# Turning the first attention head's Q and K by identity matmuls and by halves, with a mask bias in three operations

## The chip, the cores and the metric

One core of a Trainium2 chip. The metric is the device time of one execution in microseconds. The profile gives a span (first to last instruction); in nearly all runs the time is the span plus 1.8 us. Ratios are the mean time of one kernel's runs over that of the other's runs of the same rounds, so they are not quite the ratio of the medians that are quoted.

## The reference

```python
scores = scale * np.matmul(q, k.transpose(0, 1, 3, 2))      # 4 batches, 8 heads, 768 x 64
mask = window of +-1 block | first and last block | 3 sampled blocks for each of 24 query blocks
scores = np.where(mask, scores, -1e9); attn = softmax(scores)
x = attn @ v                                                 # to (4, 768, 512)
u = x + low_rank_mix(x, U, V)
out = u + np.maximum(u @ w_ch1, 0) @ w_ch2
```

## The kernel before

A pair of heads takes 12 score steps: two matmuls of 384 columns, an exponential on ACT (ScalarE), and later the product with V on PE. The mask rides in the contraction: rows 0 to 63 hold Q or K, 24 more rows hold the block's one-hot code on the query side and its bias (0 or -240) on the key side. Before the first step, Q and K of head 0 have to be loaded, cast to FP16, turned on PE, and copied to these rows. The bias has to be computed from the sampled blocks, spread over the keys by a matmul, and copied too. This start-up is what the change touches. `keep_warm` issues matmuls of zeros ("fillers") that only keep PE busy.

```python
    def first_turn(h, n):                       # n = 0: Q, 1: K
        pt = psm([P, S], FP16)
        for t in range(T):                      # 6 transposes of 128 columns
            nc.tensor.transpose(
                out=pt[0 : (h + 1) * D, t * P : (t + 1) * P],
                in_=sts[0, ("qld", "kld")[n]][:, t, 0 : h + 1].rearrange("p h d -> p (h d)"),
                identity=id16,
            )
        return pt
    def first_rows(h, n, pt, copy):             # one copy of the whole row, 768 columns
        copy(out=(qres, kres)[n][0][drows[h], h, :], in_=pt[drows[h], :])
# ... in the start-up, each engine in this order (memsets cut):
        keep_warm(8)
        nc.scalar.copy(out=qres[0][mrows[0], 0, :], in_=ohT)
        first_cast(0, 0, nc.vector.tensor_copy)
        ptq = first_turn(0, 0)
        keep_warm(1)
        prev = ms
        for r in range(3):                      # a01 = max(mask, sampled == block), 3 times
            nc.vector.scalar_tensor_tensor(...)
        nc.vector.tensor_scalar(out=bias..., scalar1=-MASK_BIAS, scalar2=MASK_BIAS, ...)
        first_rows(0, 0, ptq, nc.vector.tensor_copy)
        first_cast(0, 1, nc.scalar.copy)
        # two mask matmuls, 24 rows, 384 columns each, into pks[0], pks[1]  (cut)
        first_rows(0, 1, first_turn(0, 1), nc.scalar.copy)
        keep_warm(3)
        # four mask rows copied, (head 0, half 1) on ACT, the others on DVE  (cut)
```

The softmax here doesn't subtract the row's maximum and nothing guards it: scores larger than these inputs give would overflow.

## Time and profile before

303.17 us, median of 3 runs (302.99 to 303.46) when the prediction was made. The profiled execution had a span of 303.4 us and a time of 305.13. That is 2 us above the other three.

| stage of the profiled run | us | what leads |
|---|---|---|
| start-up | 0 to 8.8 | casts, turns, mask, copies in a chain |
| batch 0 | 8.8 to 54 | the exponentials on ACT |
| the rest | 54 to 303.4 | PE, busy nearly all the time |

The first lines below are the page's busy times. The others are from the view of three stretches: for each its length, then busy time and (in brackets) instructions of PE, of its weight loads, of DVE, ACT and POOL, then the granted clock, the DMA share and GB/s.

```profile
PE 295.6 (97%) x2760; PEld 181.1 (60%) x2760; DVE 141.6 (47%) x298; ACT 182.4 (60%) x261; POOL 49.7 (16%) x69
```

```profile
0.00:8.80 8.80, 7.61 (x26) 2.87 (x27) 5.80 (x14) 3.73 (x5) 3.16 (x11) 1.00 0.68 200
8.80:54.00 45.20, 43.12 (x588) 30.45 (x587) 28.35 (x63) 43.03 (x59) 26.34 (x35) 1.00 1.01 280
54.00:303.40 249.40, 244.86 (x2153) 147.83 (x2149) 107.49 (x223) 135.64 (x199) 20.22 (x25) 1.00 0.43 102
```

After the start-up ACT is busy 43.0 of 45.2 us, and PE about as much. Later PE alone has no room. So a gain at the start of the exponentials goes through to the end, unless something later eats it.

Now the start-up: PE, then ACT, by the timeline (start, duration of the merged group, engine, line, operation, output<-input, rows*columns of the weights, rows x columns of the moving side, count, and idle time before it with its releaser).

```profile
4.71 0.85 PE L188 MATMUL pm<-id_94,stqld 128*64 128x128 f16 x6
5.49 0.61 PE L209 MATMUL psc<-warm 128*128 128x512 f16 x1
6.03 0.50 PE L231 MATMUL pv<-small,bias 24*128 24x384 f16 x1
6.33 0.52 PE L231 MATMUL pm<-small,bias 24*128 24x384 f16 x1
6.78 0.85 PE L188 MATMUL pm<-id_94,stkld 128*64 128x128 f16 x6
7.56 1.46 PE L209 MATMUL psc<-warm 128*128 128x512 f16 x3
8.81 0.85 PE L327 MATMUL psc<-qres_102,kres_104 128*128 128x384 f16 x2
9.45 0.85 PE L188 MATMUL pm<-id_94,stqld 128*128 128x128 f16 x6
10.09 0.75 PE L327 MATMUL psc<-qres_102,kres_104 128*128 128x384 f16 x2
10.68 0.50 PE L188 MATMUL pm<-id_94,stkld 128*128 128x128 f16 x6
```

```profile
7.66 0.79 ACT L196 COPY kres_104<-pm 64x768 f16<-64x768 f16 x1 [2.47 <-PE pm L188]
8.48 0.47 ACT L241 CAST kres_104<-pm 24x384 f16<-24x384 f32 x1
9.70 0.81 ACT L333 ACTIVATE est<-psc 128x768 f16<-128x768 f32 x1 [0.74 <-PE psc L327]
10.88 3.77 ACT L333 ACTIVATE est<-psc 128x768 f16<-128x768 f32 x5 [0.37 <-PE psc L327]
```

The same six 128-column transposes take 0.85 us at 9.45 and 0.50 at 10.68; one by one their starts are 107 and 56 ns apart. PE's clock opens from half to full in between. The trace's own record of the granted clock begins its stretch of full speed at 10.61 us. The page's clock row shows 9 throughout and the view of the first stretch 1.00. Neither tells this, so it has to be read from the spacing of matmuls. The first exponential starts at 9.70, and the second waits 0.37 us for slow matmuls.

### The profile page before, as it was taken

How to read it: one execution, taken by the hardware profiler on the slowest of the kernel's cores; microseconds unless marked ns; L12 is line 12 of the kernel's file. 1: busy time of each engine (PE TensorE's matmuls, PEld its weight loads, DVE VectorE, ACT ScalarE, POOL GpSimd, SP SyncE). 2: the span in 40 equal slices, each digit the busy share in tenths (PEclk: the TensorE clock that was granted, in tenths of full speed). 3: DMA queues.
4: the chain of work that ended last, by engine and by line, in shares of the span. 5: the costliest groups of instructions: out<-in, count | busy, mean ns of one | idle time of the engine just before them, and what ended most of it. 6: DMA issues, size and time to landing. Idle time of an engine off the chain costs nothing.

```text
span 303.4 us, 6760 instructions
## 1 busy us (share of the span) xinstructions
PE 295.6 (97%) x2760; PEld 181.1 (60%) x2760; DVE 141.6 (47%) x298; ACT 182.4 (60%) x261; POOL 49.7 (16%) x69
## 2 busy tenths in 40 slices
PE   8999999999999999999999999999999999999994
PEld 3566766666666556666665556566665555665441
DVE  7466766546553533445462523446463435443121
ACT  3899999577766665777776555677776530332000
POOL 3691493222221111020201001000000000000000
PEclk9999999999999999999999999999999999999999
DMA  6999989979966476461946162431500121000111
GB/s 186 328 295 240 328 254 236 279 176 187 219 195 139 143 162 177 103 167 26 159 71 136 49 143 77 110 72 28 104 18 22 62 61 71 35 0 2 69 69 70
DMA packets 58519, 39.96 MB, mean 132 GB/s; under 512 B 40136, under 2 KB 54872, under 8 KB 58488
## 3 DMA queue, kind: packets, MB, share of 16 engines
q1 hardware_dynamic: 55764, 35.32, 44.4%
q0 software_dynamic: 2688, 4.19, 7.6%
q8 instruction: 21, 0.34, 0.4%
q14 instruction: 10, 0.08, 0.1%
q10 hardware_dynamic: 36, 0.01, 0.0%
HBM read 27.72 MB, written 6.29 MB: 112 GB/s over the span
## 4 chain that ended last, share of the span: by engine, by line
PE 89%; ACT 7%; DVE 2%; issue 1%; ACTq 0%
PE pm L447 27%; PE pm L469 27%; PE psc L327 17%; PE pv L366 10%; ACT est L333 7%; PE psc L209 2%; PE pm L388 1%; PE pm L419 1%; PE pm L188 1%; DVE xh L380 1%; DVE xf L380 0%; PE pm L465 0%; PE pm L435 0%; DVE of L477 0%; PE pm L314 0%
## 5 line engine op out<-in xcount | busy, mean ns | idle before, releaser
L333 ACT ACTIVATE est<-psc 128x768 f16<-128x768 f32 x192 | 151.5, 810 | 54.8 <-PE psc L327 53.7
L469 PE MATMUL pm<-w2t,tT 128*128 128x512 f16 x384 | 94.1, 379 | 0.0
L366 PEld LDWEIGHTS <-est 128*128 128x128 f16 x1152 | 55.4, 97 | 23.1 <-DVE xf L380 3.4
L447 PEld LDWEIGHTS <-w1t 128*128 128x128 f16 x512 | 46.3, 98 | 25.3
L457 DVE TENSOR_SCALAR tT<-pm 128x384 f16<-128x384 f32 x64 | 35.6, 556 | 51.5 <-PE pm L447 37.7
L455 ACT ACTIVATE tT<-pm 128x384 f16<-128x384 f32 x64 | 31.4, 491 | 35.8 <-PE pm L447 17.0
L469 PEld LDWEIGHTS <-tT 128*128 128x128 f16 x384 | 34.1, 98 | 30.7
L327 PE MATMUL psc<-qres_102,kres_104 128*128 128x384 f16 x192 | 47.4, 329 | 1.2 <-ACT est L333 1.0
L327 PE MATMUL psc<-qres_103,kres_105 128*128 128x384 f16 x192 | 46.7, 326 | 0.6 <-ACT est L333 0.4
L477 DVE TENSOR_TENSOR of<-xf,pm 128x512 f32<-128x512 f32 x24 | 16.4, 684 | 30.5 <-PE pm L469 30.5
L366 PE MATMUL pv<-vt_98,est 128*128 128x65 f16 x576 | 30.3, 193 | 0.2
L366 PE MATMUL pv<-vt_99,est 128*128 128x65 f16 x576 | 30.5, 193 | 0.1
L327 PEld LDWEIGHTS <-kres_104 128*128 128x128 f16 x192 | 18.2, 98 | 14.3 <-issue 2.1
L327 PEld LDWEIGHTS <-kres_105 128*128 128x128 f16 x192 | 18.1, 98 | 14.1 <-issue 0.8
L375 DVE RECIPROCAL rcp<-pv 128x6 f32<-128x6 f32 x32 | 6.2, 193 | 37.4 <-PE pv L366 37.3
L380 DVE TENSOR_TENSOR xh<-pv,rcp 128x384 f16<-128x384 f32 x32 | 17.8, 557 | 1.0
L380 DVE TENSOR_TENSOR xf<-pv,rcp 128x384 f32<-128x384 f32 x32 | 17.5, 547 | 0.0
L425 DVE TENSOR_TENSOR xf<-xf,pm 128x384 f32<-128x384 f32 x24 | 13.1, 546 | 0.0
L140 POOL CAST qst_100<-qld 128x768 f16<-128x768 f32 x5 | 4.1, 828 | 44.9 <-DMA qres_102<-qst_100 44.8
L140 POOL CAST qst_101<-qld 128x768 f16<-128x768 f32 x5 | 4.2, 831 | 43.8 <-DMA qres_103<-qst_101 43.8
L447 PE MATMUL pm<-uT_3047,w1t 128*128 128x384 f16 x32 | 10.4, 326 | 0.0
L447 PE MATMUL pm<-uT_3048,w1t 128*128 128x384 f16 x32 | 10.4, 326 | 0.0
(118 smaller groups left out, 300.4 us busy)
## 6 DMA issues: line engine op xcount, KB each, us to landing
vld<-in_v_dram SPq DMA_DIRECT2D x16, 384.0 KB, 7.2
out_dram<-of SPq DMA_DIRECT2D x24, 256.0 KB, 2.0
qld<-in_q_dram SPq DMA_DIRECT2D x15, 384.0 KB, 3.9
kld<-in_k_dram SPq DMA_DIRECT2D x15, 384.0 KB, 6.6
w1t<-in_moe_w_ch_dram POOLq DMA_DIRECT2D x4, 512.0 KB, 10.0
w2t<-in_moe_w_ch_dram POOLq DMA_DIRECT2D x4, 512.0 KB, 12.1
qld<-in_q_dram SPq DMA_DIRECT2D x2, 192.0 KB, 3.5
kld<-in_k_dram SPq DMA_DIRECT2D x2, 192.0 KB, 4.6
```

The costliest lines, as they stand in the source:

```text
L140: last = nc.gpsimd.tensor_copy(out=dst, in_=ld)
L327: nc.tensor.matmul(psc[:, c, 0:HS], kT[:, h, g * P : (g + 1) * P], qT[:, h, c * HS : (c + 1) * HS], start=True, stop=True,)
L333: nc.scalar.activation(out=est.rearrange("k (c n) -> k c n", c=2), in_=psc[:, :, 0:HS], func=AF.Exp, scale=0.125,)
L366: nc.tensor.matmul(pav[:, sc, :], est[:, sc * P : (sc + 1) * P], vts[self.b % 2][:, head, g, 0 : D + 1], start=(g == 0 and sc == 0), stop= ...
L375: nc.vector.reciprocal(out=rcp, in_=pav[:, :, D])
L380: nc.vector.tensor_tensor(out=dst, in0=pav[:, :, 0:D], in1=rcp[:, :, None].broadcast_to([P, T, D]), op=ALU.mult,)
L425: nc.vector.tensor_add(out=xf, in0=xf, in1=pu)
L447: nc.tensor.matmul(pt, w1t[:, cc, jj * P : (jj + 1) * P], bt.uT[cc][:, c * HS : (c + 1) * HS], start=(cc == 0), stop=(cc == NCC - 1),)
L455: nc.scalar.activation(out=dst, in_=pt, func=AF.Relu)
L457: nc.vector.tensor_scalar_max(out=dst, in0=pt, scalar1=0.0)
L469: nc.tensor.matmul(hold[sc], bt.tT[jj][:, sc * P : (sc + 1) * P], w2t[:, jj, :], start=(b > 0 and jj == 0), stop=(jj == NJJ - 1),)
L477: nc.vector.tensor_add(out=of, in0=bt.xf[:, sc, :], in1=hold[sc])
```

## The change

Turn Q and K of the first head by ordinary matmuls against the identity, into FP32 PSUM, in two halves of 384 columns; put K ahead of the mask and drop the filler before it; copy the halves on DVE and ACT side by side; shorten the last fillers; compute the bias in three operations. A likely reason for matmuls in place of transposes: the Trainium skill ("TensorE: Matmul & The Clock Gate", Part 4) says that transposes do not count as PE activity for the clock.

```diff
-        [ms_np.view(np.float16), ...]
+        [((ms_np - 1.0) * -MASK_BIAS).view(np.float16), ...]
-    def first_turn(h, n):                      # 6 transposes into one FP16 tile
+    def first_turn(h, n, c):                   # half c: 3 matmuls into an FP32 tile
+            nc.tensor.matmul(pt[0:D, j * P : (j + 1) * P],
+                sts[0, ("qld", "kld")[n]][:, 3 * c + j, h], id16,
+                start=(j == 0), stop=(j == 2), skip_group_check=True)
 ...
         keep_warm(8)
         first_cast(0, 0, nc.vector.tensor_copy)
-        ptq = first_turn(0, 0)
-        keep_warm(1)
-        (bias in 4 operations)
-        first_rows(0, 0, ptq, nc.vector.tensor_copy)
-        first_cast(0, 1, nc.scalar.copy)
-        (two mask matmuls)
-        first_rows(0, 1, first_turn(0, 1), nc.scalar.copy)
-        keep_warm(3)
-        (four mask rows, one on ACT)
+        first_turn(0, 0, 0)
+        first_turn(0, 0, 1)
+        (bias in 3 operations: compare with all 3 samples, reduce by max, scale and max)
+        first_cast(0, 1, nc.scalar.copy)
+        first_turn(0, 1, 0)
+        first_row(0, 0, nc.vector.tensor_copy)
+        first_row(0, 1, nc.scalar.copy)
+        mask_half(0)
+        first_row(1, 0, nc.scalar.copy)
+        first_turn(0, 1, 1)
+        mask_half(1)
+        keep_warm(2, 256)
+        mask_row(0, 0, nc.vector.tensor_copy)
+        first_row(1, 1, nc.vector.tensor_copy)
+        (the other three mask rows on DVE)
```

More of the change, by code (lines that the diff above doesn't have):

```diff
@@ L69 @@
     small_np = np.concatenate(
-        [ms_np.view(np.float16), ii[:, None].astype(np.float32).view(np.float16), ohT_np],
+        [
+            ((ms_np - 1.0) * -MASK_BIAS).view(np.float16),
+            ii[:, None].astype(np.float32).view(np.float16),
+            ohT_np,
+        ],
         axis=1,
@@ L174 @@
     bias = consts.tile([P, 2, D], FP16)
-    a01 = consts.tile([P, NB], FP32)
     for vt in vts:
@@ L183, in first_cast @@
         copy(out=sts[0, nm][:, :, h], in_=lds[nm][:, h])
-    def first_turn(h, n):
-        pt = psm([P, S], FP16)
-        for t in range(T):
-            nc.tensor.transpose(
-                out=pt[0 : (h + 1) * D, t * P : (t + 1) * P],
-                in_=sts[0, ("qld", "kld")[n]][:, t, 0 : h + 1].rearrange("p h d -> p (h d)"),
-                identity=id16,
-            )
-        return pt
-    def first_rows(h, n, pt, copy):
-        copy(out=(qres, kres)[n][0][drows[h], h, :], in_=pt[drows[h], :])
+    first_out = {}
+    def first_turn(h, n, c):
+        if n == 1:
+            pt = psm([P, HS], FP32)
+        elif c == 0:
+            pt = pw[:, 1, 0:HS]
+        else:
+            pt = pscp.tile([P, 2, 512], FP32, tag="psc", name="psc")[:, 0, 0:HS]
+        first_out[n, c] = pt
+        for j in range(3):
+            nc.tensor.matmul(
+                pt[0:D, j * P : (j + 1) * P],
+                sts[0, ("qld", "kld")[n]][:, 3 * c + j, h],
+                id16,
+                start=(j == 0), stop=(j == 2), skip_group_check=True,
+            )
     with tc.manual_schedule(
@@ L205, with keep_warm, mask_half @@
         pw = pscp.tile([P, 2, 512], FP32, tag="psc", name="psc")
-        def keep_warm(n):
+        def keep_warm(n, cols=512):
             for _ in range(n):
-                nc.tensor.matmul(pw[:, 0], warm[:, 0:P], warm, start=True, stop=True)
-        keep_warm(8)
-        nc.scalar.copy(out=qres[0][mrows[0], 0, :], in_=ohT)
-        first_cast(0, 0, nc.vector.tensor_copy)
-        ptq = first_turn(0, 0)
-        keep_warm(1)
-        prev = ms
-        for r in range(3):
-            nc.vector.scalar_tensor_tensor(
-                out=a01[0:NB], in0=sb[0:NB, :, r, 0], scalar=iota,
-                in1=prev, op0=ALU.is_equal, op1=ALU.max,
-            )
-            prev = a01[0:NB]
-        nc.vector.tensor_scalar(
-            out=bias[0:NB, :, 0:NB], in0=a01[0:NB, None].broadcast_to([NB, 2, NB]),
-            scalar1=-MASK_BIAS, scalar2=MASK_BIAS, op0=ALU.mult, op1=ALU.add,
-        )
-        first_rows(0, 0, ptq, nc.vector.tensor_copy)
-        first_cast(0, 1, nc.scalar.copy)
+                nc.tensor.matmul(
+                    pw[:, 0, 0:cols], warm[:, 0:P], warm[:, 0:cols], start=True, stop=True
+                )
         pks = [psvp.tile([P, HS], FP32, tag="pv", name="pv"), psm([P, HS], FP32)]
-        for c in range(2):
+        def mask_half(c):
             nc.tensor.matmul(
@@ L236, with mask_row @@
             )
-        first_rows(0, 1, first_turn(0, 1), nc.scalar.copy)
-        keep_warm(3)
-        for h in range(2):
-            for c in range(2):
-                (nc.scalar.copy if (h, c) == (0, 1) else nc.vector.tensor_copy)(
-                    out=kres[0][mrows[h], h, c * HS : (c + 1) * HS], in_=pks[c][mrows[h]]
-                )
-        nc.vector.tensor_copy(out=qres[0][mrows[1], 1, :], in_=ohT)
+        def mask_row(h, c, copy):
+            copy(out=kres[0][mrows[h], h, c * HS : (c + 1) * HS], in_=pks[c][mrows[h]])
@@ new lines, in first_row @@
+        def first_row(n, c, copy):
+            copy(
+                out=(qres, kres)[n][0][drows[0], 0, c * HS : (c + 1) * HS],
+                in_=first_out[n, c][0:D],
+            )
+        keep_warm(8)
+        nc.scalar.copy(out=qres[0][mrows[0], 0, :], in_=ohT)
+        first_cast(0, 0, nc.vector.tensor_copy)
+        first_turn(0, 0, 0)
+        first_turn(0, 0, 1)
+        eq = consts.tile([P, NB, 3], FP32)
+        a01 = consts.tile([P, NB], FP32)
+        nc.vector.tensor_scalar(
+            out=eq[0:NB], in0=sb[0:NB, :, :, 0], scalar1=iota, scalar2=-1.0,
+            op0=ALU.is_equal, op1=ALU.add,
+        )
@@ new lines @@
+        nc.vector.tensor_reduce(
+            out=a01[0:NB], in_=eq[0:NB], axis=mybir.AxisListType.X, op=ALU.max
+        )
+        nc.vector.scalar_tensor_tensor(
+            out=bias[0:NB, :, 0:NB], in0=a01[0:NB, None].broadcast_to([NB, 2, NB]),
+            scalar=-MASK_BIAS, in1=ms[:, None].broadcast_to([NB, 2, NB]),
+            op0=ALU.mult, op1=ALU.max,
+        )
+        first_cast(0, 1, nc.scalar.copy)
+        first_turn(0, 1, 0)
+        first_row(0, 0, nc.vector.tensor_copy)
+        first_row(0, 1, nc.scalar.copy)
@@ new lines, with last_turn @@
+        mask_half(0)
[5 more added lines that the diff above has]
+        first_row(1, 1, nc.vector.tensor_copy)
+        mask_row(0, 1, nc.vector.tensor_copy)
+        mask_row(1, 0, nc.vector.tensor_copy)
+        mask_row(1, 1, nc.vector.tensor_copy)
+        nc.vector.tensor_copy(out=qres[0][mrows[1], 1, :], in_=ohT)
+    def last_turn(n):
+        pt = psm([P, S], FP16)
+        for t in range(T):
+            nc.tensor.transpose(
+                out=pt[:, t * P : (t + 1) * P],
+                in_=sts[0, ("qld", "kld")[n]][:, t].rearrange("p h d -> p (h d)"),
+                identity=id16,
+            )
+        nc.vector.tensor_copy(
+            out=(qres, kres)[n][0][drows[1], 1, :], in_=pt[drows[1], :]
+        )
@@ L246, in first_front @@
     def first_front(n):
         first_cast(1, n, nc.gpsimd.tensor_copy)
-        first_rows(1, n, first_turn(1, n), nc.vector.tensor_copy)
+        last_turn(n)
     def second_set():
```

## The prediction

> **What bounds the kernel now.** The busy table gives PE 97% of the 303.4 us span, ACT and DVE 60% and 47%. The chain of waits has four stages. Up to about 9.7 us it is start-up. From there to about 54 us the softmax exponentials on ACT lead (0.81 us each, starting every 0.7 to 0.8 us). From 54 us the matmuls follow without a gap. The change touches only the start-up, so a gain is what it takes off the start of the exponentials; I see no stall later that would swallow it (the POOL casts of the next pairs finish ahead of their use).
>
> **Before, from the timeline.** Q cast ends 4.65; six Q transposes 4.72 to 5.56; bias by four DVE operations 4.57 to 5.56; mask matmuls end 6.53 and 6.85; six K transposes 6.78 to 7.63; ACT copies the whole K row (0.79 us) until 8.46; three 512-column filler matmuls hold PE until 8.81; first scores 8.81; first exponential 9.70. The second starts only at 10.88, 0.37 us late, because Q transposes and scores run at half clock: 512-column matmuls start 427 ns apart, 128-column ones 107 ns; after 10.6 us 56 ns.
>
> **Costs of the change.** Three bias operations instead of four: about 5.45 instead of 5.56 (estimate from 0.24 us per operation plus 48 more elements). K no longer stands behind filler and mask: its cast ends at 5.19, so half 0 of K is turned by 5.88 and mask half 0 by about 6.25. Copies from FP32 PSUM cost more: 0.55 us for 384 columns on DVE, as 768 FP16 columns cost now; but DVE and ACT share them. DVE: Q half 0 until 6.05, mask row until 6.84. ACT: Q half 1 until 6.1, K half 0 until 6.6. Data of the first scores ready at 6.9 instead of 8.5. PE's order (two matmul turns, two masks, two 256-column fillers, 0.21 us each at half clock) frees it at about 7.25. So the first scores start about 1.55 us earlier. The other mask rows and K half 1 end on DVE by 9.2, before they are needed.
>
> **Clock.** The Trainium skill ("TensorE: Matmul & The Clock Gate", Part 4) says that transposes don't count as PE activity, and Part 1 that the clock opens after a busy window of about 3.4 us. This trace fits: matmuls from 1.19 us, with 12 transposes among them, opened it only at 10.6. With real matmuls throughout it should open near 7.2, one window earlier. Then scores take 0.16 us each half, the second exponential follows the first at once (about 7.7 and 8.4), and the gain at the second is 2.4 us. If the clock still opens at 10.6, the second starts at 9.4, and the third is held again: about 0.9 us stay.
>
> **Predicted time.** Two thirds for the early clock: 300.7; else 302.2. I say 301.0, range 300.3 to 302.4. Chances: faster by over 2% 0.01, within 2% 0.98, slower 0.01.
>
> **What would show it.** Timeline: first scores near 7.2 (confirming the shorter chain), first exponential near 7.7, no gap before the second, matmul starts 56 ns apart for 128 columns before 8.5 us (confirming the clock). Chain of waits: filler and scores at the start, no ACT copy of K. From 54 us on the same durations, all shifted.
>
> **What would make it wrong.** Column- or row-weighted activity, so that 64-column and 24-row matmuls don't count either; a clock window of another phase; POOL's second K cast (waits for its DMA, ended 8.16) or pair 1's casts (10.56) becoming what PE waits for, since PE takes them in order; the mask row copies on DVE longer than read; the schedule after 54 us not passing the shift on.

## The result

302.56 us, median of 6 runs (302.19 to 302.66), against 303.31 (302.99 to 305.11, 6 runs) before: ratio 0.9965, 95% interval 0.994 to 0.9989. The class is "same", as forecast, but the time lies outside the predicted range (302.4 at most), and the gain is 0.75 us where 2.2 were forecast.

The profile, taken alone, says the opposite: its span fell from 303.4 to 300.4 us, 3 us, rather more than forecast. First the busy times and the stretches, then PE, ACT and one line of DVE, as above.

```profile
PE 292.7 (97%) x2758; PEld 180.2 (60%) x2758; DVE 142.4 (47%) x299; ACT 181.7 (60%) x261; POOL 49.6 (17%) x69
```

```profile
0.00:6.70 6.70, 5.50 (x24) 2.35 (x25) 5.13 (x13) 3.47 (x5) 2.40 (x9) 1.00 0.63 179
6.70:52.00 45.30, 43.23 (x594) 30.52 (x593) 30.70 (x67) 43.38 (x59) 28.27 (x38) 1.00 1.01 285
52.00:300.40 248.40, 243.92 (x2144) 147.28 (x2141) 106.61 (x221) 134.88 (x198) 18.91 (x23) 1.00 0.43 104
```

```profile
4.72 0.79 PE L200 MATMUL psc<-id_94,stqld 128*64 128x128 f16 x6
5.35 0.35 PE L200 MATMUL pm<-id_94,stkld 128*64 128x128 f16 x3
5.63 0.33 PE L225 MATMUL pv<-small,bias 24*128 24x384 f16 x1
5.89 0.35 PE L200 MATMUL pm<-id_94,stkld 128*64 128x128 f16 x3
6.18 0.33 PE L225 MATMUL pm<-small,bias 24*128 24x384 f16 x1
6.44 0.39 PE L218 MATMUL psc<-warm 128*128 128x256 f16 x2
6.70 0.48 PE L371 MATMUL psc<-qres_102,kres_104 128*128 128x384 f16 x2
7.02 0.50 PE L281 MATMUL pm<-id_94,stqld 128*128 128x128 f16 x6
```

```profile
5.55 0.47 ACT L236 CAST qres_102<-psc 64x384 f16<-64x384 f32 x1 [0.26 <-PE psc L200]
5.92 0.47 ACT L236 CAST kres_104<-pm 64x384 f16<-64x384 f32 x1
7.22 7.42 ACT L377 ACTIVATE est<-psc 128x768 f16<-128x768 f32 x10 [0.83 <-PE psc L371]
```

```profile
6.00 0.56 DVE L233 CAST kres_104<-pv 24x384 f16<-24x384 f32 x1 [0.16 <-PE pv L225]
```

Everything in the forecast chain is there, even earlier: scores at 6.70 us (forecast 7.25), first exponential 7.22 (7.7), no gap before the next, the clock open at 5.32 us. The stretches are cut at round times, so their lengths compare only roughly (45.2 and 45.3 us, 249.4 and 248.4 us). Exponential by exponential the two traces show it better: the third of the 192 starts 2.97 us earlier than before, the 49th 2.93, the last 2.94. In this pair of profiles the gain went through. It is the base that was wrong: the profile of before had 2 us to lose that most runs of the kernel before do not have.

### The profile page after: what moved, and what is told of

The parts are those of the page before. It is cut to its first block, busy times and chain, and to the rows that moved or that the text cites. A ratio compares the mean times of both kernels' runs of the same rounds, so it can differ in the third digit from the quotient of the medians. Undisturbed runs are those within 1.5% of the kernel's fastest.

```text
span 300.4 us, 6759 instructions
## 1 busy us (share of the span) xinstructions
PE 292.7 (97%) x2758; PEld 180.2 (60%) x2758; DVE 142.4 (47%) x299; ACT 181.7 (60%) x261; POOL 49.6 (17%) x69
## 4 chain that ended last, share of the span: by engine, by line
PE 89%; ACT 7%; DVE 2%; issue 1%; ACTq 0%
PE pm L491 28%; PE pm L513 28%; PE psc L371 17%; PE pv L410 10%; ACT est L377 7%; PE pm L432 1%; PE pm L463 1%; PE psc L218 1%; DVE xh L424 1%; DVE xf L424 0%; PE pm L509 0%; PE pm L479 0%; PE psc L200 0%; DVE of L521 0%; PE pm L358 0%
```

## The experiments

Fourteen runs, five rounds each. Besides the runs of these kernels, 55 runs of the kernel before are counted here (each chip's list once): 49 lie between 302.93 and 303.67, six between 304.91 and 305.11. The five runs of b_again are among them. The profiled execution of before (305.13) is not in these lists; by its time it belongs with the six.

**1. The kernel before, again (b_again), no edit.**

> The kernel before, unchanged. Theory A: the profiled run of before (time 305.1, clock opened at 10.6 us) was a rare one; most runs (303.0 to 303.5) open the clock earlier, by 7.2 us or before. Then most spans here are 301.2 to 301.7, and if the profile falls in such a run it shows 56 ns between 128-column matmuls before 8.5 us, first exponential near 8.3 to 9.0 and second at most 0.8 us behind it. Rival B: most runs open at 10.6 as the profiled one, and its extra 2 us came later in the execution; then a profile with span near 301.4 still shows the second exponential near 10.9 and the clock opening near 10.6.

Measured: 303.36 us median (303.05 to 303.43, 5 runs); profile with a span of 301.3 us. Its clock was open at 5.25 us. The chain of waits of this profile, in order of time (start, us, engine and line):

```profile
5.48 0.32 PE psc L210
5.80 0.27 PE pv L232
6.07 0.16 PE pm L232
6.23 0.47 PE pm L189 x6
6.70 0.02 issue
6.72 0.80 ACT kres L197
7.52 0.05 issue
7.56 0.51 PE psc L328 x2
8.08 0.02 issue
8.10 2.22 ACT est L334 x3
```

This is the base that the prediction should have used: filler (L210), mask, turn of K, ACT's copy of the whole K row (0.80 us), scores at 7.56, first exponential at 8.10, the following ones without a gap. The last three fillers are not in the chain: here they end before the copy does. Against it, at nearly the same clock opening (5.25 and 5.32 us), the changed kernel starts its exponentials at 7.22, 0.88 us earlier, and its span is 0.85 us shorter (301.27 and 300.42). Theory A holds, rival B falls.

**2. What the late clock costs (b_late, a_late).** Both kernels with `keep_warm(8)` cut to `keep_warm(2)`, so that the clock has to open late.

```diff
-        keep_warm(8)
+        keep_warm(2)
```

> The kernel before with 2 of its first 8 fillers, so that no window before 7.3 us is busy and the clock has to open late (7.3 to 10.7 us). Theory (clock phase made the profiled run of before 2 us longer than the others): exponentials start near 9.7 and the second near 10.9 where it opens after 10 us, time 304 to 305.2. If the late clock is not what cost the 2 us, the time stays at 303.0 to 303.5.

> The changed kernel with 2 of its first 8 fillers. With the clock late (7.3 to 10.7 us): first exponential 7.9 to 8.2, second up to 9.4; time 302.8 to 304.2, that is about 1 us below b_late and 0.3 to 1.6 above the changed kernel. It says what the chain alone is worth when both are cold; if the identity matmuls wake the clock better than transposes, it opens earlier here than in b_late by 1 us or more.

Measured: b_late 305.18 us (304.68 to 305.74), a_late 304.58 (304.15 to 304.89), 6 runs each. The clock opened at 10.33 and 10.08 us in the profiles. The exponentials in b_late, then in a_late:

```profile
9.81 0.81 ACT L333 ACTIVATE est<-psc 128x768 f16<-128x768 f32 x1 [0.75 <-PE psc L327]
10.79 3.77 ACT L333 ACTIVATE est<-psc 128x768 f16<-128x768 f32 x5 [0.18 <-PE psc L327]
```

```profile
8.40 0.81 ACT L377 ACTIVATE est<-psc 128x768 f16<-128x768 f32 x1 [1.97 <-PE psc L371]
9.68 4.83 ACT L377 ACTIVATE est<-psc 128x768 f16<-128x768 f32 x6 [0.47 <-PE psc L371]
```

b_late reproduces the profiled run of before (9.70 and 10.88, with 303.3 against 303.4 us of span). So the late clock was the 2 us: between the profiles of before and b_again the difference is 2.07 us at the second exponential and 2.09 at the end. With both clocks late the changed kernel keeps 0.6 us of medians, and 0.90 us between the spans of the two profiles (303.28 and 302.38). a_late came out above its range (at most 304.2 was expected), and its clock opened no more than 0.25 us before b_late's, where 1 us was expected if identity matmuls woke it better. That is one profile each.

**3. Identity matmuls or transposes (a_T).** The changed kernel with transposes into FP16 PSUM put back, halves and order kept.

```diff
-            nc.tensor.matmul(pt[0:D, j * P : (j + 1) * P], sts[...][:, 3 * c + j, h], id16, ...)
+            nc.tensor.transpose(out=pt[0:D, j * P : (j + 1) * P],
+                in_=sts[...][:, 3 * c + j, h], identity=id16)
```

> The changed kernel with transposes (FP16 PSUM) again in place of the identity matmuls of the first head; order and halves kept. If transposes do not count as activity of PE, the clock opens later than in the changed kernel in part of the runs: spans spread from 300.5 to about 302.5, mean time 0.3 to 1 us above the changed kernel. If they count like matmuls, times equal the changed kernel's 302.2 to 302.7 within 0.2 us, and the cheaper FP16 copies change nothing, since the first mask row waits for its matmul.

Measured: 302.49 us (302.14 to 302.77, 5 runs), the changed kernel's within 0.1 us. This part of the change is worth nothing that these runs can see. (In the profile a_T's first exponential is even 0.09 us earlier, at 7.13, but by its third, at 8.87 against 8.62, the lead is lost, as PE turned K of the second head only at 8.02; see experiment 8.)

**4. Do transposes count as activity (a_fillT)?** As a_T, with 16 transposes in place of the last four of the eight fillers.

```diff
-        keep_warm(8)
+        keep_warm(4)
+        for _ in range(16):
+            nc.tensor.transpose(out=pw[:, 0, 0:64].bitcast(FP16), in_=warm[:, 0:P], identity=id16)
```

> As a_T, and besides 16 of the fillers' time (1.7 us) spent on 128-column transposes in place of four 512-column matmuls: from about 2.9 to 5.6 us PE does transposes nearly alone. If transposes do not count, no window that ends before about 8 us is busy, so the clock opens at 8 to 11 us in every run: scores at half clock, first exponential 0.3 us later and second over 1.1 us behind the first; time 303.5 to 304.8. If they count, as a_T within 0.2 us.

Measured: spans 300.4 to 300.9 us in all 6 runs, as the changed kernel's. (The times are 302.52 to 303.70, median 303.27: in four runs, and only of this kernel, the time was 2.6 to 2.9 us above the span instead of 1.8. Why is open, so spans are compared here.) In the profile:

```profile
3.06 1.86 PE L242 MATMUL psc<-id,warm 128*128 128x128 f16 x16
4.85 0.63 PE L200 MATMUL psc<-id,stqld 128*64 128x128 f16 x6
```

The clock opened at 5.12 us, in the midst of the second line, after 2 us of transposes alone. In the 3.41 us before that, matmuls fill some 34% by their starts and transposes 56%. Fillers alone, at 76% of a window, did not open the clock in the profile of before (0.37 to 3.78 us, experiment 5). So transposes, as this kernel issues them, count. (The trace lists them as MATMUL and does not show their mode.)

**5. Then what does not (a_fill24, a_fill64)?** The changed kernel with its last four of eight first fillers contracting over 24 rows, as the mask matmuls do, or with 64 columns of weights, as the turns do.

```diff
-        keep_warm(8)
+        keep_warm(4)
+        for _ in range(4):                       # a_fill24; a_fill64: pw[0:D, 0], warm[:, 0:D], warm
+            nc.tensor.matmul(pw[:, 0], warm[0:NB, 0:P], warm[0:NB], start=True, stop=True)
```

> The changed kernel with the last four of its first eight fillers contracting over 24 rows instead of 128 (same length, from 2.9 to 4.6 us). If matmuls over 24 rows do not count as activity, a window that ends before about 8 us is too empty, and the clock opens at 8 to 11 us in most runs: first exponential 7.9 to 8.3, second 0.9 us or more behind, spans 301.8 to 303. If they count, spans are the changed kernel's 300.3 to 300.9.

> The same with 64 columns instead of 24 rows: four fillers whose weights have 64 columns. If 64-column matmuls count in full, spans are the changed kernel's 300.3 to 300.9; if they count half or not, late clocks as for a_fill24, in part of the runs or most.

Measured: a_fill24 304.61 us (304.06 to 304.84), all 6 runs late, the clock open only at 12.33 us in the profile; a_fill64 302.62 (302.50 to 302.98), open at 5.48, none of its 6 runs late (two spans, 301.1 and 301.2, lie just above the expected 300.9). PE and ACT of a_fill24:

```profile
3.01 1.88 PE L243 MATMUL psc<-warm 24*128 24x512 f16 x4
```

```profile
8.52 0.81 ACT L379 ACTIVATE est<-psc 128x768 f16<-128x768 f32 x1 [1.97 <-PE psc L373]
9.80 0.81 ACT L379 ACTIVATE est<-psc 128x768 f16<-128x768 f32 x1 [0.47 <-PE psc L373]
```

Matmuls over 24 rows do not keep the clock, those with 64 columns do. Whether 24 rows count for nothing, or only for too little, these runs do not tell.

This fits the late run of before. The records' stretches of full speed are 290.133, 293.546 or 296.960 us long, that is 85, 86 or 87 times 3.413 us, so the clock seems to be decided once in 3.41 us. This agrees with the window of 3413 ns that runs on freely, of which the Trainium skill ("TensorE: Matmul & The Clock Gate", Part 1) tells. In the late run one decision fell at 10.61 - 3.41 = 7.20 us. From 3.78 to 7.20 PE ran matmuls for some 85% of the time by their starts, mask matmuls included, and for 67% without them. One earlier, the window from 0.37 to 3.78 has 76%, because PE starts at 1.19 us. Neither opened the clock. A window with 80% did (b_kfirst below, opened at 3.93). These shares are estimates from the starts in the traces. They give no threshold: a_fast (experiment 9) opened its clock after a window, from 7.04 to 10.46 us, with 72%. That the masks and the place of the windows are the whole cause of all six late runs is inferred. Besides the run of 305.13, only a late run of b_bias3 was profiled; its missed windows look the same (85% with the masks and 67% without, and 71% in the one before).

**6. The bias alone (b_bias3).** The kernel before with the three-operation bias.

```diff
-        prev = ms
-        for r in range(3): nc.vector.scalar_tensor_tensor(...)   # and tensor_scalar
+        nc.vector.tensor_scalar(out=eq...); nc.vector.tensor_reduce(...); nc.vector.scalar_tensor_tensor(...)
```

> The kernel before with only the bias in three operations. The bias gets ready 0.28 us earlier (5.28 against 5.56), but the filler ahead of the mask matmul holds PE until 5.92 and the K transposes and the copy of the whole K row follow; both theories expect at most 0.1 to 0.2 us gain, which is hardly clear of noise; a gain of over 0.4 us would say that the bias bounded the start.

Measured: 304.13 us (302.82 to 305.08, 6 runs): three runs at 304.9 to 305.1 with the late clock, three at 302.82 to 303.38. The latter are hardly below before's. The bias alone gives nothing clear of noise, and it slows nothing either: its late profile has the mask matmul at 6.035 us, as the late profile of before has (6.033).

**7. The order alone (b_kfirst), and without the last fillers (b_kfirst0).** Whole rows, transposes, old bias; K's turn moved ahead of the mask.

```diff
         ptq = first_turn(0, 0)
-        keep_warm(1)
 ...
+        ptk = first_turn(0, 1)
         (two mask matmuls)
-        first_rows(0, 1, first_turn(0, 1), nc.scalar.copy)
+        first_rows(0, 1, ptk, nc.scalar.copy)
-        keep_warm(3)                              # this line in b_kfirst0 only
```

> The kernel before with one thing moved: the six K transposes go ahead of the two mask matmuls, and the filler between Q and mask is gone; whole rows, transposes, old bias. Theory (order): in a usual run of before the first scores wait for the ACT copy of the whole K row (7.56 us), which starts late because K is turned after filler, bias and mask; turned first, the copy ends near 6.75, the three fillers free PE near 6.9, first exponential near 7.4, time 302.6 to 302.8 (0.5 to 0.7 us below before). Rival (halves): it is the halves, shared by DVE and ACT, that shorten the start; then this gains under 0.3 us.

> b_kfirst without its three fillers before the scores. In b_kfirst's profile the data were ready at 6.64 us and the fillers held PE until 6.80; so first scores near 6.68, first exponential near 7.2 with an early clock. Theory (order and fillers are the gain with an early clock, halves help only while the clock is late): 302.35 to 302.5 with an early clock (0.15 below b_kfirst), 302.7 to 303.0 with a later one. If halves matter in themselves, it stays at b_kfirst's 302.5 to 303.1.

Measured: b_kfirst 303.03 us (302.51 to 303.10, 6 runs; ratio 0.9981, interval 0.9956 to 1.0006, so unclear by itself, and above the 302.6 to 302.8 that was expected); b_kfirst0 302.49 (302.31 to 302.82, 5 runs; ratio 0.9972). Each kernel spreads by 0.5 to 0.7 us, so lowest is compared with lowest and highest with highest:

| kernel | lowest | highest | below before |
|---|---|---|---|
| before, 49 runs not late | 302.93 | 303.67 | |
| b_kfirst: order | 302.51 | 303.10 | 0.4 to 0.6 |
| b_kfirst0: and no last fillers | 302.31 | 302.82 | 0.6 to 0.9 |
| changed kernel, 11 runs | 302.05 | 302.66 | 0.9 to 1.0 |

By this table the order gives about half, the shorter fillers perhaps a quarter, and halves, sharing and bias what is left. But the table mixes runs of several chips, and two other readings differ. In b_kfirst's own rounds the nine runs of before that were not late average 303.08 us and b_kfirst 302.89: only 0.19 us, within the "under 0.3" of the rival (halves). In the profiles the first exponential starts at 8.10 us (b_again), 7.32 (b_kfirst), 7.31 (b_kfirst0) and 7.22 (changed kernel): there the order has 0.78 of the 0.88 us, though b_kfirst's clock also opened earlier, at 3.93 us. So how the gain divides among order, fillers and halves stays open; together, without the last fillers, order gave 0.72 us in b_kfirst0's own rounds (302.54 against 303.26, means).

**8. The changed kernel, again (a_again), no edit.**

> The changed kernel, unchanged, for its spread. Theory (gain is the shorter chain alone, about 0.8 us, and the clock's phase adds 0 to 0.5 us to either kernel): 302.1 to 302.7 in nearly all runs, 0.6 to 0.9 us below the usual runs of before. If the identity matmuls guard against the late clock, no run lies near 304.2; if not, one or two in thirty would, which six runs can't settle.

Measured: 302.48 us (302.05 to 302.55, 5 runs), ratio 0.9964 (0.9945 to 0.9983). The result stands. None of the changed kernel's 11 runs is late; at before's rate of 6 in 55 one would be expected, so whether it is safer stays open. Its own mask matmuls have 24 rows too.

This profile also shows a stall that takes part of the gain. The clock opened at 5.43 us and the first exponential started at 7.26, nearly as in the first profile of the changed kernel (5.32 and 7.22), yet the span is 300.69 us and not 300.42. From its chain of waits:

```profile
3.04 4.31 DMA kld<-in_k_dram
7.40 0.52 POOL stkld L187
7.96 0.51 PE pm L282 x6
```

K of the second head landed at 7.35 us, POOL cast it at 7.40 (6.79 in the first profile), and PE could turn it only at 7.96. Against b_again the lead fell from 0.84 us at the first exponential to 0.67 at the third and 0.48 at the ninth.

**9. Tries for a faster version (a_best, a_fast, a_fast2).** a_best is a_T with the first mask matmul ahead of K, no last fillers, and K's turn of the second head at score step 3. a_fast also computes the bias before the Q cast, with the memsets of the second pair's rows on POOL, 6 first fillers instead of 8, and both turns of the second head later; a_fast2 brings these memsets back to DVE and has 7 first fillers.

```diff
+        (bias operations, mask_half(0), mask_half(1) before first_turn(0, 0, 0))
-        for res in (*qres, *kres): nc.vector.memset(res, 0.0)
+        for res in (qres[1], kres[1]): nc.gpsimd.memset(res, 0.0)   # a_fast; DVE, later, in a_fast2
-        at(1, lambda: first_front(1))
+        at(1, cast of K, head 1); at(3, lambda: last_turn(1))
```

> From a_T (transposes, FP16 PSUM, halves): mask half 0 ahead of the turn of K, no fillers before the scores, and the turn of K of the second head two score steps later. The chain then is bias (5.28), mask matmul (end near 5.75), mask row on DVE (near 6.35) against K half 0 on ACT (near 6.4): first scores near 6.45, first exponential near 7.0, 0.2 us ahead of the changed kernel; time 302.2 to 302.5. Not lower than the changed kernel's 302.2 to 302.7 by over 0.3 us.

> A try for a version faster than both: from a_T, the bias computed before the Q cast (its data land at 2.6 us, Q at 4.0), the memsets of the second pair's rows on POOL, mask matmuls ahead of Q, the turns of the second head two steps later. What is left is K: landing 4.6, cast to 5.2, turned to 5.7, copied by halves to 6.3. First scores near 6.3, first exponential near 6.85: 0.3 to 0.4 us ahead of the changed kernel: 301.8 to 302.2. If POOL's second casts or the loads of the next pair then hold PE or ACT, the gain shrinks to 0.1 or nothing.

> a_fast mended: in its profile the bias comparison on DVE took 2.5 us and ended with POOL's memsets; here no memset lies on POOL, one goes on DVE behind the bias, one behind the first mask rows. If the overlap with POOL was the cause, the comparison takes 0.23 us again, bias ready near 3.5, K bounds the start (cast 5.2, turned 5.7, copied 6.3): first scores near 6.3, first exponential near 6.85, spans near 300.0, time 301.7 to 302.1, 0.3 us below the changed kernel's. If the loads of the next pair hold the exponentials from there on, 302.1 to 302.5.

Measured: a_best 302.52 us (302.02 to 303.59), no better than the changed kernel; its profile starts the exponentials at 7.55 us, not near 7.0, with the clock open at 6.33. a_fast 304.55 (302.69 to 305.30), with the clock open at 10.46 in the profile. DVE, then POOL of a_fast:

```profile
2.74 2.51 DVE L246 TENSOR_SCALAR eq<-sb,small 24x72 f32<-24x72 int32 x1
```

```profile
2.51 1.39 POOL L214 MEMSET qres<- 128x1536 f16 x1
3.83 1.38 POOL L214 MEMSET kres<- 128x1536 f16 x1
```

A comparison that takes 0.23 us elsewhere took 2.51 and ended within 0.05 us of POOL's last memset. The Trainium skill ("SBUF — State Buffer", section "SBUF: two separate sides") describes an exclusive lock on a port pair that POOL shares with DVE operations of some kinds, among them those in a mode that uses two ports. This trace agrees, but does not show in which mode the comparison ran. a_fast2 cured it: the comparison took 0.25 us and the bias was ready at 3.47. But it came to 303.60 (302.01 to 304.89): the two mask matmuls now stand at 4.3 us, where fillers had kept the clock, and in the profile it opened at 10.64, the scores running slow from 7.45. (The window from 3.81 to 7.22 has 78% with the masks and 60% without; that this is why is inferred.) One run in six, at 302.01, matched the changed kernel's best (302.05). No version was clearly faster than it.

## Why the prediction was wrong

- **The chain: right in kind, too large in size.** K first, rows in halves on two engines, shorter fillers. Scores were forecast at 7.25 and came at 6.70 us. In the usual run of before they stand at 7.56, not at the profiled run's 8.81, so the chain gives 0.86 us where the text counted 1.55. Its fallback, "about 0.9 us stay" if the clock is late in both kernels, is what the profiles of b_late and a_late show (0.90 us of span).
- **The clock: the step that failed.** "Then scores take 0.16 us each half, the second exponential follows the first at once (about 7.7 and 8.4), and the gain at the second is 2.4 us." The timing came true (7.22 and 7.93 us). The gain did not. The step took it for granted that before always opens its clock late, at 10.6 us; in a usual run of before it opened at 5.25, and the second exponential starts at 8.81 (b_again), not at 10.88. That term measured 0.88 us.
- **How it slipped in.** The text took 303.17 us, the median, and subtracted from it what it had read from a profile whose own time was 305.13. It checked "what bounds" in that profile and never whether the run was a usual one. Subtracting 2.4 us from 305.13 would have given 302.7, close to the measured 302.56 (by luck in part, as the two profiles differ by 2.95 us): the difference between the early and the late runs of before was counted as a gain of the change.
- **"Transposes don't count as PE activity": wrong here.** The late clock "fit" this, with 12 transposes among the matmuls. a_fillT refutes it; by a_fill24 the gap was more likely the 24-row mask matmuls. The text had named row-weighted activity as a possible error, but only for the changed kernel.
- **No stall later that swallows the gain: right for one pair of profiles, not always.** Between b_again and the first profile of the changed kernel the span's gain (0.85 us) is that of the first exponential (0.88). In a_again's profile 0.84 us at the first exponential shrank to 0.58 us of span, because PE waited for POOL's second K cast. The text had named this wait among what would make it wrong.
- **Three bias operations: right in kind and worthless.** The bias was ready at 5.28 instead of 5.56 us (forecast 5.45), and b_bias3 shows no gain clear of noise.
- **Class:** within 2%, as forecast.

## What to carry to other kernels

Before reading a gain from a profile, compare the profiled run's own time with the other runs; if it is off by as much as the gain you hope for, find out what that run did differently first. In a start-up of a few microseconds, order the work so that the longest chain of turn and copy starts first; here one moved block, with one filler dropped, brought the first exponential 0.78 us forward in a profile, though its own runs leave the gain in time unclear. For matmuls that are meant to keep the clock up, 24 rows were too few here and 128 were enough; nothing in between was tried. Moving low-row matmuls into a stretch that kept the clock up can cost more than the chain saves, as a_fast2 suggests.

## What the Trainium skill lacked or had wrong

- "TensorE: Matmul & The Clock Gate", Part 4, says that transpose mode "doesn't count as PE-busy the same way". Here a clock opened at 5.12 us after 2 us of transposes alone (a_fillT), with spans as with matmuls (300.4 to 300.9 us). The trace does not show the mode of these instructions.
- The same page, Part 1, describes the window by time and busyness, not by rows. Matmuls over 24 rows did not count, or too little (a_fill24: open at 12.33 us, all 6 runs late); matmuls with 64 columns of weights did (5.48 us).
- Part 1's window of 3413 ns is confirmed by the records: 290.133, 293.546 and 296.960 us of full speed are 85, 86 and 87 of them. The page lets the moment at which the clock opens vary by about 500 ns from run to run; here it lay at 5.25 us in one profile of before and at 10.61 in another, and the late clock cost about 2 us (before: 302.93 to 303.67, or 304.91 to 305.11 in 6 of 55).
- "SBUF — State Buffer" says (section "SBUF: two separate sides") that DVE and GpSimd share a port pair that one of them holds for its whole instruction. It does not say that POOL's next instruction can keep out a DVE operation that is already waiting. Here a DVE operation of 0.23 us began at 2.74 us, within POOL's first memset, and ended at 5.25, after the second one that began at 3.83.
